# Halves of w1 by columns, and the second search's keys between row splits, in a routed expert kernel

## The chip, the cores and the metric

The kernel runs on one core of a Trainium2 chip. The core has five engines with a queue each: TensorE (PE, with its weight loads shown apart as PEld), VectorE (DVE), ScalarE (ACT), GpSimd (POOL) and SyncE (SP), and 16 DMA engines that they share. Each engine works through its own queue in the order in which the program was written, and waits at an instruction until what it needs is there. The metric is the time of one execution in device microseconds.

## The reference

The program computes an attention with a window of 32 and 32 global positions per head, and sends each of its 4608 rows of 512 numbers to one of eight experts. Each expert takes 576 rows: the highest gate values choose first, and who finds an expert full goes on.

```python
logits = x @ w_gate
order = np.argsort(-logits.flatten())
for idx in order:
    tok, e = (int(idx) // E, int(idx) % E)
    if assigned[tok] >= 0 or counts[e] >= cap:
        continue
    assigned[tok] = e
    counts[e] += 1
for e in range(E):
    mask = assigned == e
    h = np.maximum(x[mask] @ w1[e], 0.0)
    out[mask] = h @ w2[e]
```

w1 is 512 x 1024 and w2 1024 x 512 for each expert.

## The kernel before

**Stages.** Attention and the gate logits take the first 212 us and leave x in device memory (`xd`). Then the routing finds, one expert at a time, which expert fills first and which rows it gets. `search_alone` does this for the first expert with nothing beside it. `search` does it for each later one, in pieces that are laid between the matmuls of the expert that runs at that time. Before a search, `key` and `own` work out from the logits `L` what it compares: ten VectorE instructions that write r_m, r_v, r_f, r_v, r_u, r_mv, r_hi, r_G (these are `key`) and r_mo, r_oh (`own`). `key` is a generator that yields between five groups of them; `setup` runs `key` and then `own`. A search then does eight rounds: matmuls `R<-r_oh,r_G` on TensorE, r_ce on VectorE, matmuls with `big`, a scan r_pm, and the next r_G. At its end `widx` holds the row numbers for gathering this expert's weights, and a little later `idx` (made from the matmul `R<-c,r_w`) those of its token rows.

**An expert.** `ffn` computes with matmuls of float32r, each product as three: high x high, high x low and low x high parts. w1 is gathered into two tiles `w1r`, w2 into two tiles `w2r`, and the 576 token rows into five tiles `xg` (128, 128, 128, 128 and 32 rows), all by indirect DMAs that POOL issues (L895). A split takes a 128 x 512 piece: ACT copies it to the high part (w1h, w2h; L911) and VectorE subtracts to get the low part (w1l, w2l). w1 has eight pieces: j runs over 4 row blocks x 2 column halves, an even j being the first column half. `trans_x` transposes one row tile on TensorE, ACT makes xh from it (L936) and VectorE xl. For w1, eight column blocks f of 128 each, in two halves of rows, take 12 matmuls into an `H` tile (three buffers), from which ACT makes hh and VectorE hl. For f below 4 only the first column half of w1 is used. Then come the matmuls into `Y`, from which ACT makes y, and POOL scatters y to the output.

**What sets the order.** Within an expert, a table of due pieces (`at`, `step`, `force`) with an estimated clock of the program places splits, transpositions, gathers and the parts of the next search between the matmuls, when the program is built. The times it uses are constants in the code; `V.busy` and `V.now` are its estimates of where VectorE and TensorE stand. The pieces for even j carry the tag "a" and may come once the running expert is past its f = 4 (`half`), those for odd j the tag "b" and may come once it is done with w1. A piece of w1 is due when the gather it is read from is thought to have landed.

**Around the change.** w1 is stored so that each gather brings two of the four row blocks with all 1024 columns: pieces j = 0..3 read the first gather, j = 4..7 the second. For the first expert the order is written out at the end of `experts`: both w1 gathers as soon as `widx` is there, the row gathers after `idx`, both w2 gathers; on TensorE `HEAT` = 14 matmuls of `ident` with itself (`keep_warm`), then the five transpositions with three more such matmuls between them; on VectorE first the whole `setup` for the second search, then four w1l, then the xl. The odd pieces of w1 and all of w2 are left to the table.

Of the kernel before, what the change touches and what calls it, by code (L numbers as in the profile page):

```python
# [8 lines left out]
F32 = mybir.dt.float32  # L9
# [12 lines left out]
E = 8  # L22
FF = 1024
# [851 lines left out]
def experts(ctx, tc, A, xd, ident, rt, out):  # L875
    nc = tc.nc
    wp = ctx.enter_context(tc.tile_pool(name="wp", bufs=1))
    st = ctx.enter_context(tc.tile_pool(name="st", bufs=2))
    ps = ctx.enter_context(tc.tile_pool(name="fps", bufs=1, space=PSUM))
    w1h = [wp.tile([128, FF], F32R, name=f"w1h{c}") for c in range(4)]  # L880
    w1l = [wp.tile([128, FF], F32R, name=f"w1l{c}") for c in range(4)]
# [12 lines left out]
    def gather(dst, src, off, idx):  # L894
        nc.gpsimd.indirect_dma_start(out=dst, out_offset=None, in_=src, element_offset=off,  # L895
                                     in_offset=bass.IndirectOffsetOnAxis(ap=idx, axis=0))

    def load_w1(ph):
        raws = []
        for k in range(2):  # L900
            raw = st.tile([128, 2, FF], F32, name="w1r", bufs=2)
            gather(raw.rearrange("p a b -> p (a b)"), A["w1"], k * E * 128 * 2 * FF, rt.widx[ph][:, :1])
            raws.append(raw)
        return raws

    def load_w2(ph):
        for k in range(2):
            gather(w2r[k].rearrange("p a b -> p (a b)"), A["w2"], k * E * 128 * 4 * DM, rt.widx[ph][:, :1])

    def split(hi, lo, raw, eng):  # L910
        nc.scalar.activation(hi, raw, AF.Copy)  # L911
        eng.tensor_tensor(lo, raw, hi, op=ALU.subtract)

    def split_w1(raws, j, eng):
        q = slice(512 * (j % 2), 512 * (j % 2) + 512)
        split(w1h[j // 2][:, q], w1l[j // 2][:, q], raws[j // 4][:, (j // 2) % 2, q], eng)

    def split_w2(j, eng):
        split(w2h[j], w2l[j], w2r[j // 4][:, j % 4], eng)
# [1 line left out]
    def load_x(ph):  # L921
        xg = []
        for t in range(5):
            n = sizes[t]
            g = st.tile([128, DM], F32, name="xg", bufs=5)
            gather(g[:n], xd, 0, rt.idx[ph][:n, t:t + 1])
            xg.append(g)
        return xg

    def trans_x(xg, t):  # L930
        n = sizes[t]
        p = ps.tile([128, 4, 128], F32, name="H", bufs=3)
        for d in range(4):
            nc.tensor.transpose(p[:, d, :n], xg[t][:n, 128 * d:128 * d + 128], ident[:n, :n])  # L934
        q = slice(128 * t, 128 * t + n)
        nc.scalar.activation(xh[:, :, q], p[:, :, :n], AF.Copy)  # L936
        V.tensor_tensor(xl[:, :, q], p[:, :, :n], xh[:, :, q], op=ALU.subtract)
# [9 lines left out]
    fill, todo, raw1 = [], [], {}  # L947
    done, cur, mid, wrote = [False], [0], [-1], [0.0]

    def pool_op(ns, nbytes=0):  # L950
        pool[0] = max(pool[0], V.now) + ns
        if nbytes:
            dma[0] = max(dma[0], pool[0] + 1800) + nbytes / 360.0
            return dma[0] + 300
        return pool[0]

    def calm():
        return V.busy < V.now + AHEAD
# [13 lines left out]
    def at(tag, t, f, cond=None):  # L972
        todo.append((tag, t, cond, f))
# [27 lines left out]
    def low1(p, j):  # L1001
        split_w1(raw1[p], j, V)
# [2 lines left out]
        split_w2(j, V)  # L1005

    def get_w1(p, half):
        raw1[p] = load_w1(p)
        r = [pool_op(1040, 1 << 20) for _ in range(2)]
        for i in range(4):  # L1010
            at(f"a{p}", r[i // 2], lambda j=2 * i: low1(p, j), lambda: (half or mid[0] == p - 1) and calm())
        for i in range(4):
            at(f"b{p}", r[i // 2], lambda j=2 * i + 1: low1(p, j), lambda: mid[0] == p - 1 and calm())

    def get_x(p):
        xg = load_x(p)
# [22 lines left out]
    def ffn(ph):  # L1039
# [4 lines left out]
        if nxt < E:  # L1044
            at(f"g{nxt}", t0, lambda: get_w1(nxt, half), lambda: nxt in rt.widx and not pending(f"b{ph}"))
            at(f"h{nxt}", t0, lambda: get_x(nxt), lambda: nxt in rt.idx and (mid[0] == ph or V.now > t0 + TX))
            at(f"v{nxt}", t0, lambda: get_w2(nxt), lambda: mid[0] == ph and nxt in rt.widx and
               (not pending(f"h{nxt}") or V.now > t0 + TW))
# [54 lines left out]
    raws = None  # L1103
# [4 lines left out]
    def keep_warm(n):  # L1108
        for _ in range(n):
            nc.tensor.matmul(heat[:, :128], ident, ident, start=True, stop=True)  # L1110

    for _ in rt.phase(0):
        if raws is None and 0 in rt.widx:
            raws = load_w1(0)
    xg = load_x(0)
    load_w2(0)
    keep_warm(HEAT)
    raw1[0] = raws
    for _ in rt.setup(slice(0, 34)):
        pass  # L1120
    for j in range(4):
        split_w1(raws, 2 * j, nc.vector)
    for t in range(5):
        trans_x(xg, t)
        if t < 4:
            keep_warm(3)
    V.now = V.busy
    for j in range(4):
        at("b0", 0, lambda j=j: low1(0, 2 * j + 1), calm)
# [7 lines left out]
def _blocks(a, x, g):  # L1137
    pad = np.zeros_like(np.take(x, range(32), axis=a))
    bl = [pad] + np.split(x, NW, axis=a) + [pad]
    out = []  # L1140
    for i, b in enumerate(bl):
        out.append(b)
        if i % 2 == 0 and i < NW + 1:
            out.append(g)
    return np.concatenate(out, axis=a)


def _layout(q_l, k_l, v_l, q_g, k_g, v_g, moe_w_gate, moe_w1, moe_w2):
    f = np.float32
    qT = np.concatenate([q_l, q_g], axis=2).transpose(0, 1, 3, 2)  # L1150
    kT = _blocks(3, k_l.transpose(0, 1, 3, 2), k_g.transpose(0, 1, 3, 2))
    qk = np.concatenate([qT, kT], axis=3).reshape(B, NP, 2 * D, QW + KW)
    vs = _blocks(2, v_l, v_g)
    st = [32 * ((3 * j + 1) // 2) for j in range(NW)]
    vs = np.concatenate([vs, np.ones_like(vs[..., :1])], axis=3)
    vw = np.stack([vs[:, :, t:t + 128] for t in st[::2]], axis=3)
    vw = vw.reshape(B, NP, 2, 128, NW // 2, D + 1).transpose(0, 1, 3, 2, 4, 5).reshape(B, NP, 128, NW * (D + 1))
    w1 = moe_w1.reshape(E, 2, 2, 128, FF).transpose(1, 0, 3, 2, 4).reshape(2 * E * 128, 2 * FF)
    w2 = moe_w2.reshape(E, 2, 4, 128, DM).transpose(1, 0, 3, 2, 4).reshape(2 * E * 128, 4 * DM)
    wg = np.zeros((128, 4, 32), f)  # L1160
    wg[:, :, :E] = moe_w_gate.reshape(4, 128, E).transpose(1, 0, 2)[:, :, ::-1]
    mask = np.full((128, NB, 128), 0.0, f)
    i = np.arange(32)
    for j in range(NW):
        for w, bk in enumerate([j - 1, j, None, j + 1] if j % 2 else [j - 1, None, j, j + 1]):
            if bk is not None:
                t = 32 * bk + i
                ok = (np.abs(t[None] - 32 * j - i[:, None]) <= 32) & (t >= 0) & (t < SL)
                h = 32 * (j % 4)
                mask[h:h + 32, j // 4, 32 * w:32 * w + 32] = np.where(ok, 0.0, -3.0e37)  # L1170
    p = np.arange(128)
    cf = np.zeros((128, CF), f)
    cf[:, 0:8] = 1 + np.arange(8)
    cf[:, 13] = p + 1024
    ids = np.zeros((128, 34), int)
    for J in range(32):
        ids[:, J] = (J // 4) * S + SG + 128 * (J % 4) + p
    for J in (32, 33):
        ids[:, J] = (4 * (J - 32) + p // 32) * S + p % 32
    cf[:, 20:88] = np.stack([ids // 64, ids % 64], -1).reshape(128, 68)  # L1180
    cf[:, 88:216] = np.arange(128)[None]
    cf[:, 216:344] = -(p[:, None] >= p[None]).astype(f)
    cf[:, 344:472] = 1
    cf[:, 472:480] = (p[:, None] % 8 == np.arange(8)[None])
    cf[:, 480:512] = (p[:, None] % 32 == np.arange(32)[None])
    h = p % 16
    cf[:, 512:640] = (h[:, None] < 9) & (h[:, None] % 2 == np.arange(128)[None] // 64)
    cf[:, 640:645] = (h[:, None] // 2 == np.arange(5)[None]) * np.where(p % 32 < 16, 64, 1)[:, None]
    k = np.arange(16)
    for it in range(NIT):  # L1190
        cf[:, CTAB + 16 * it:CTAB + 16 * it + 16] = k * 16.0 ** (3 - it)
    cf[:, CFIN:CFIN + 128] = (256 + 16 * k[:, None] + 1 + np.arange(E)[None]).reshape(1, 128)
    cf[:, CMISC:CMISC + 32] = CU * (p[:, None] % 32 == np.arange(32)[None])
    a = dict(qk=qk, vw=vw, w1=w1, w2=w2, wg=wg.reshape(128, 128), mask=mask.reshape(128, 512),
             ident=np.eye(128, dtype=f), cf=cf)
    return {n: np.ascontiguousarray(x) for n, x in a.items()}
# [15 lines left out]
```

## Time and profile before

| what | value |
|---|---|
| median of 3 runs | 719.35 us (718.57 to 726.27) |
| profiled execution | 716.33 us |
| its span | 714.6 us, 23883 instructions |
| TensorE busy | 658.5 us, 92% |
| VectorE busy | 477.3 us, 67% |
| ScalarE busy | 320.8 us, 45% |
| GpSimd busy | 221.7 us, 31% |
| first expert matmul | 251.72 us |

The span is cut below by stretches of time. A group's busy time can hold overlaps, since a matmul's weight load and the end of the one before it run beside it; the start times of neighbouring rows tell the pace. A row of a timeline has the start in us, the length in us, the engine, the line, the instruction with output and inputs, how many were merged into it, and in brackets the idle time of the engine before it with what ended it. The name after an arrow in the brackets is the last releaser that the profile saw.

### The profile page before, as it was taken

The page shows a single profiled execution, that of the slowest core. Times are in us where ns is not written, and L with a number is a line of the kernel's source. Part 1 is how long each engine was busy: PE and PEld are TensorE (multiplying, and loading weights), DVE is VectorE, ACT ScalarE, POOL GpSimd, SP SyncE. Part 2 cuts the span into 40 slices and gives each one's busy share as a digit, 9 for nine tenths or more (in the row PEclk, how much of TensorE's full clock was granted, in tenths as well). Part 3 has the DMA queues.
Part 4 walks back from the last instruction along what each step waited for, and adds up shares of the span by engine and source line. Part 5 has one row for each costly group of instructions (what it writes and reads, how often), then busy time and mean ns, then how long its engine had stood idle before and what let it go on. Part 6 is the DMA issues. An engine that isn't in the chain of part 4 may idle for free.

```text
span 714.6 us, 23883 instructions
## 1 busy us (share of the span) xinstructions
PE 658.5 (92%) x9972; PEld 538.9 (75%) x9972; DVE 477.3 (67%) x1766; ACT 320.8 (45%) x870; POOL 221.7 (31%) x248
## 2 busy tenths in 40 slices
PE   7888898898993699999999999999999999999997
PEld 5666676676772598779789779878978877988985
DVE  3779777687777878767767777767776774640510
ACT  5867867776840243343244234234333342641421
POOL 3665546554510500430240241142043035312002
PEclk9999999999995599999999999999999999999999
DMA  8788878887310620730540351261063065331001
GB/s 281 244 270 274 273 247 258 282 268 246 134 68 2 216 84 1 266 96 2 209 139 17 144 177 42 86 213 66 2 241 121 2 250 177 116 118 49 16 16 48
DMA packets 39580, 102.86 MB, mean 144 GB/s; under 512 B 4912, under 2 KB 14384, under 8 KB 35376
## 3 DMA queue, kind: packets, MB, share of 16 engines
q1 hardware_dynamic: 29232, 49.95, 21.6%
q0 software_dynamic: 10240, 51.39, 20.4%
q8 instruction: 78, 1.28, 0.7%
q14 instruction: 30, 0.25, 0.1%
HBM read 83.49 MB, written 17.83 MB: 142 GB/s over the span
## 4 chain that ended last, share of the span: by engine, by line
PE 45%; DVE 4%; issue 3%; DMA 3%; POOL 1%; ACT 1%; POOLq 0%; DVEq 0%; ACTq 0%
PE Y L1090 19%; PE H L1062 19%; PE R L617 3%; PE H L934 2%; DVE w2l L546 2%; PE Y L1080 2%; DMA xg<-xd,idx 2%; DMA out_dram<-y,idx 1%; DVE r_G L546 1%; ACT w2h L911 1%; POOL xg L895 1%; DVE r_pm L546 0%; PE Y L1096 0%; DVE hl L546 0%; POOL w1r L895 0%
## 5 line engine op out<-in xcount | busy, mean ns | idle before, releaser
L1062 PE MATMUL H<-xh,w1h 128*128 128x272 f32 x512 | 151.3, 296 | 1.8 <-DVE hl L546 1.4
L1062 PE MATMUL H<-xh,w1l 128*128 128x272 f32 x512 | 150.1, 293 | 0.0
L1062 PE MATMUL H<-xl,w1h 128*128 128x272 f32 x512 | 149.9, 293 | 0.0
L1064 ACT ACTIVATE hh<-H 128x272 fp32r<-128x272 f32 x128 | 50.9, 398 | 130.1 <-PE H L1062 125.7
L1090 PE MATMUL Y<-w2h,hh 128*128 128x512 f32 x256 | 103.9, 406 | 0.0
L1090 PE MATMUL Y<-w2l,hh 128*128 128x512 f32 x256 | 102.7, 401 | 0.0
L1090 PE MATMUL Y<-w2h,hl 128*128 128x512 f32 x256 | 102.4, 400 | 0.0
L1062 PEld LDWEIGHTS H<-xh,w1h 128*128 128x128 f32 x512 | 96.5, 188 | 5.2 <-DVE hl L546 2.2
L1062 PEld LDWEIGHTS H<-xl,w1h 128*128 128x128 f32 x512 | 96.4, 188 | 0.6
L1062 PEld LDWEIGHTS H<-xh,w1l 128*128 128x128 f32 x512 | 96.4, 188 | 0.3
L941 POOL DMA_INDIRECT out_dram<-y,idx x40 | 40.2, 1006 | 137.4 <-ACT y L1032 79.3
L173 ACT ACTIVATE p<-p,nm 128x128 f32<-128x128 f32 x256 | 78.1, 397 | 10.4 <-DVE nm L168 10.4
L168 DVE CUSTOM_DVE_ANT_0 p<-S,mask 128x128 f32<-128x128 f32 x256 | 56.8, 286 | 28.0 <-PE S L83 25.9
L546 DVE SCALAR_TENSOR_TENSOR hl<-H,hh 128x272 fp32r<-128x272 f32 x128 | 54.4, 433 | 23.6 <-ACT h L1066 12.7
L546 DVE TENSOR_TENSOR w2l<-w2r,w2h 128x512 fp32r<-128x512 f32 x64 | 43.1, 686 | 37.4 <-ACT w2h L911 37.0
L895 POOL DMA_INDIRECT w1r<-in_w_dram,widx x16 | 15.7, 981 | 165.9 <-DVE r_a L546 124.3
L83 PE MATMUL S<-qk 64*32 64x128 f32 (+2 forms) x2240 | 53.9, 293 | 12.6 <-issue 6.1
L1032 ACT ACTIVATE y<-Y 128x512 f32<-128x512 f32 (+1 forms) x40 | 23.2, 594 | 92.1 <-PE Y L1090 65.9
L119 POOL COPY vw<-vw 64x1040 f32<-64x1040 f32 x32 | 33.6, 1049 | 88.3 <-DMA vw<-in_vw_dram 61.4
L1090 PEld LDWEIGHTS Y<-w2h,hh 128*128 128x128 f32 x256 | 48.2, 188 | 15.7 <-issue 5.9
L911 ACT ACTIVATE w1h<-w1r 128x512 fp32r<-128x512 f32 x64 | 36.4, 622 | 47.4 <-DVE r_ohg L546 27.5
L1090 PEld LDWEIGHTS Y<-w2h,hl 128*128 128x128 f32 x256 | 48.2, 188 | 10.1 <-issue 0.2
(176 smaller groups left out, 1215.7 us busy)
## 6 DMA issues: line engine op xcount, KB each, us to landing
vw<-in_vw_dram SPq DMA_DIRECT2D x64, 260.0 KB, 3.8
qk<-in_qk_dram SPq DMA_DIRECT2D x64, 216.0 KB, 3.5
qk<-in_qk_dram SPq DMA_DIRECT2D x32, 272.0 KB, 4.1
xd<-xs SPq DMA_DIRECT2D x28, 256.0 KB, 3.5
xd<-xs SPq DMA_DIRECT2D x1, 1024.0 KB
xg<-xd,idx POOLq DMA_INDIRECT x40, 3.6
out_dram<-y,idx POOLq DMA_INDIRECT x40, 2.7
cf<-in_cf_dram SPq DMA_DIRECT2D x1, 512.0 KB
```

The costliest lines, as they stand in the source:

```text
L83: s.last = op(o, w, x, **kw)
L119: nc.gpsimd.tensor_copy(od[0:64], ev[64:128])
L168: nc.vector.tensor_tensor_reduce(s.p[:, c, :], s.st[:, c, :], mask[:, c, :], -SCALE, BIG, ALU.add, ALU.min, s.nm[:, c:c + 1])
L173: nc.scalar.activation(s.p[:, c, :], s.p[:, c, :], AF.Exp, bias=s.nm[:, c:c + 1], scale=-1.0)
L546: return op(*args, **kw)
L895: nc.gpsimd.indirect_dma_start(out=dst, out_offset=None, in_=src, element_offset=off, in_offset=bass.IndirectOffsetOnAxis(ap=idx, axis=0))
L911: nc.scalar.activation(hi, raw, AF.Copy)
L941: nc.gpsimd.indirect_dma_start(out=out, out_offset=bass.IndirectOffsetOnAxis(ap=rt.idx[ph][:n, t:t + 1], axis=0), in_=y[:n], in_offset=None)
L1032: nc.scalar.activation(y[:n], p[:n], AF.Copy)
L1062: nc.tensor.matmul(p, w[d][:, fs], x[:, d, q], start=(d + k == 0), stop=(d + k == 5))
L1064: nc.scalar.activation(hh[:, f, q], p, AF.Relu)
L1090: nc.tensor.matmul(p, h[:, f, q], w[f], start=(f + k == 0), stop=(f + k == 9))
```

## The change

w1 is laid out in device memory so that the first gather brings the first 512 columns of all four row blocks, and the second the other 512. The even pieces j then read the first gather and the odd pieces the second, for every expert. For the first expert only the first gather is issued when `widx` is there; the second follows the five row gathers in POOL's queue, ahead of w2's. The second search's `setup` is no longer run ahead of the w1l subtractions: its first four steps go behind the first four row tiles, one each, and the rest behind the fifth. In the table the "a" pieces are due with the first gather and the "b" pieces with the second.

```diff
-    def load_w1(ph):
-        raws = []
-        for k in range(2):
-            raw = st.tile([128, 2, FF], F32, name="w1r", bufs=2)
-            gather(raw.rearrange("p a b -> p (a b)"), A["w1"], k * E * 128 * 2 * FF, rt.widx[ph][:, :1])
-            raws.append(raw)
-        return raws
+    def load_w1(ph, k):
+
+        raw = st.tile([128, 4, FF // 2], F32, name="w1r", bufs=2)
+        gather(raw.rearrange("p a b -> p (a b)"), A["w1"], k * E * 128 * 2 * FF, rt.widx[ph][:, :1])
+        return raw
...
-        split(w1h[j // 2][:, q], w1l[j // 2][:, q], raws[j // 4][:, (j // 2) % 2, q], eng)
+        split(w1h[j // 2][:, q], w1l[j // 2][:, q], raws[j % 2][:, j // 2], eng)
...
-        raw1[p] = load_w1(p)
+        raw1[p] = [load_w1(p, k) for k in range(2)]
         r = [pool_op(1040, 1 << 20) for _ in range(2)]
         for i in range(4):
-            at(f"a{p}", r[i // 2], lambda j=2 * i: low1(p, j), lambda: (half or mid[0] == p - 1) and calm())
+            at(f"a{p}", r[0], lambda j=2 * i: low1(p, j), lambda: (half or mid[0] == p - 1) and calm())
         for i in range(4):
-            at(f"b{p}", r[i // 2], lambda j=2 * i + 1: low1(p, j), lambda: mid[0] == p - 1 and calm())
+            at(f"b{p}", r[1], lambda j=2 * i + 1: low1(p, j), lambda: mid[0] == p - 1 and calm())
...
-            raws = load_w1(0)
+            raws = [load_w1(0, 0)]
     xg = load_x(0)
+    raws.append(load_w1(0, 1))
     load_w2(0)
     keep_warm(HEAT)
     raw1[0] = raws
-    for _ in rt.setup(slice(0, 34)):
-        pass
     for j in range(4):
         split_w1(raws, 2 * j, nc.vector)
+    setup = rt.setup(slice(0, 34))
     for t in range(5):
         trans_x(xg, t)
         if t < 4:
             keep_warm(3)
+            next(setup, None)
+    for _ in setup:
+        pass
     V.now = V.busy
```

Three places show what this does to the queues. The first is VectorE ahead of the first expert: r_G, r_mo and r_oh end the second search's keys, w1l are the low parts of w1's first column half, xl those of the row tiles. Before:

```order
L546 TENSOR_TENSOR r_G<-r_hi,cf 128x544
L546 SCALAR_TENSOR_TENSOR r_mo<-r_asgv,r_mv 128x34
L546 TENSOR_TENSOR r_oh<-r_v,r_mo 128x272
L912 TENSOR_TENSOR w1l_5374<-w1r,w1h_5370 128x512
L912 TENSOR_TENSOR w1l_5375<-w1r,w1h_5371 128x512
L912 TENSOR_TENSOR w1l_5376<-w1r,w1h_5372 128x512
L912 TENSOR_TENSOR w1l_5377<-w1r,w1h_5373 128x512
L546 TENSOR_TENSOR xl<-H,xh 128x4x128 x4
L546 TENSOR_TENSOR xl<-H,xh 128x4x32
```

The same place now, from behind the second row tile on:

```order
L546 TENSOR_TENSOR r_v<-L,r_m 128x272
L546 TENSOR_SCALAR r_f<-r_m 128x34
L546 TENSOR_TENSOR xl<-H,xh 128x4x128
L546 TENSOR_TENSOR r_v<-r_v,wtb 128x272
L546 TENSOR_TENSOR r_u<-r_f,r_m 128x34
L546 TENSOR_TENSOR xl<-H,xh 128x4x128
L546 TENSOR_REDUCE r_mv<-r_v 128x34
L546 TENSOR_SCALAR r_hi<-r_u 128x34
L546 TENSOR_TENSOR xl<-H,xh 128x4x32
L546 TENSOR_TENSOR r_G<-r_hi,cf 128x544
L546 SCALAR_TENSOR_TENSOR r_mo<-r_asgv,r_mv 128x34
L546 TENSOR_TENSOR r_oh<-r_v,r_mo 128x272
```

The keys moved from ahead of the w1l to between and behind the xl, and r_oh from ahead of everything to the end.

The second place is TensorE at the start of the first expert: the last transposition, the first expert matmuls (H), and the first matmul of the second search (R), which reads r_G and r_oh. Before:

```order
L1110 MATMUL Y<-ident 128x128 x3
L934 MATMUL H<-ident,xg 128x32 x4
L1062 MATMUL H<-xh,w1h_5370 128x272
L617 LDWEIGHTS r_G
L617 MATMUL R<-r_oh,r_G 32x16
```

Now:

```order
L932 MATMUL H<-ident,xg 128x32 x4
L1060 MATMUL H<-xh,w1h_5370 128x272
L1060 MATMUL H<-xl,w1h_5370 128x272
L1060 MATMUL H<-xh,w1l_5374 128x272
L1060 MATMUL H<-xh,w1h_5371 128x272
L617 LDWEIGHTS r_G
L617 MATMUL R<-r_oh,r_G 32x16
```

The search begins behind four expert matmuls instead of one.

The third place is ACT in the second expert's Y stage, where it makes the third expert's w1h between the evacuations y of the second. Before:

```order
L1032 ACTIVATE y<-Y 32x512
L911 ACTIVATE w1h_5370<-w1r 128x512
L911 ACTIVATE w1h_5371<-w1r 128x512
L911 ACTIVATE w1h_5372<-w1r 128x512
L911 ACTIVATE w1h_5373<-w1r 128x512
L1032 ACTIVATE y<-Y 128x512
```

Now:

```order
L1030 ACTIVATE y<-Y 32x512
L909 ACTIVATE w1h_5370<-w1r 128x512
L909 ACTIVATE w1h_5371<-w1r 128x512
L909 ACTIVATE w1h_5372<-w1r 128x512
L1030 ACTIVATE y<-Y 128x512
L909 ACTIVATE w1h_5373<-w1r 128x512
```

One split moved behind the next y; in the first expert's Y stage, where the fourth split stood behind that y, the third now does too. From the third expert on the later experts' Y stages repeat, in the main, the order that the expert before them had, and in the sixth expert's the row gathers of the seventh go ahead of its w2 gathers in POOL's queue.

More of the change, by code (lines that the diff above doesn't have):

```diff
@@ L1157, in _layout @@
     vw = vw.reshape(B, NP, 2, 128, NW // 2, D + 1).transpose(0, 1, 3, 2, 4, 5).reshape(B, NP, 128, NW * (D + 1))
-    w1 = moe_w1.reshape(E, 2, 2, 128, FF).transpose(1, 0, 3, 2, 4).reshape(2 * E * 128, 2 * FF)
+    w1 = moe_w1.reshape(E, 4, 128, 2, FF // 2).transpose(3, 0, 2, 1, 4).reshape(2 * E * 128, 2 * FF)
     w2 = moe_w2.reshape(E, 2, 4, 128, DM).transpose(1, 0, 3, 2, 4).reshape(2 * E * 128, 4 * DM)
```

## The prediction

> **What bounds the kernel now.** I read the page's busy shares first, then the table of busy time by stretch, then TensorE's waits, and last the timeline around the start of the first expert. The stretch rows give the span's start and end, its length, then busy us (and instructions) of PE, PEld, DVE, ACT and POOL, the granted clock, the DMA share and GB/s.
> ```profile
> 240.87:251.72 10.85, 10.85 (x73) 10.69 (x72) 8.20 (x20) 4.07 (x8) 5.81 (x7) 0.73 0.80 270
> 251.72:714.60 462.88, 452.85 (x3814) 377.99 (x3812) 290.82 (x772) 167.51 (x400) 105.08 (x103) 1.00 0.29 103
> ```
> ```profile
> PE H L934 <- DMA xg<-xd,idx: 1.5, 2, 1.1
> PE H L1062 <- DVE hl L546: 1.4, 5, 0.5
> PE R L617 <- DVE r_G L546: 1.1, 3, 0.4
> ```
> From 251.72 us, where the first expert's matmuls begin, TensorE is busy 452.85 of 462.88 us at full clock: 97.8%. Its waits that the profile names there (us in total, times, longest) come to 4.0 us. So behind 251.72 no edit that leaves the matmuls alone can win over 10 us, and by the named waits not over 4.0. An added wait in TensorE's queue, on the other hand, goes straight to the end. The question is what happens at 240.87 to 254, which the change rewrites.
> ```profile
> 240.87 6.13 PE L1110 MATMUL Y<-ident 128*128 128x128 f32 x28
> 246.84 0.60 PE L934 MATMUL H<-ident,xg 128*128 128x128 f32 x4
> 251.36 0.43 PE L934 MATMUL H<-ident,xg 32*128 32x32 f32 x4
> 251.72 0.39 PE L1062 MATMUL H<-xh,w1h 128*128 128x272 f32 x1
> 252.04 0.28 PE L617 MATMUL R<-r_oh,r_G 128*32 128x16 f16 x17
> 252.26 0.40 PE L1062 MATMUL H<-xl,w1h 128*128 128x272 f32 x1
> 252.74 0.29 PE L1062 MATMUL H<-xl,w1h 128*128 128x272 f32 x1
> ```
> TensorE (start, length, instruction) runs the 14 warming matmuls (28 records) without a break from 240.87 to the first row transposition at 246.84, and no idle time stands in any of these rows: nothing that arrives earlier can start the transpositions earlier, because the warming matmuls stand ahead of them in the queue and are not changed. The first part of the second search (R) runs at 252.04 behind one expert matmul.
>
> **The gathers.** The landing rows give minimum, median and maximum from issue, first for w1's two gathers of the first expert, then for the row gathers up to 262 us.
> ```profile
> 234.20 1.17 POOL L895 DMA_INDIRECT w1r<-in_w_dram,widx  x1 [0.78 <-POOL widx L766]
> 235.68 0.95 POOL L895 DMA_INDIRECT w1r<-in_w_dram,widx  x1 [0.31 <-issue]
> 246.30 0.96 POOL L895 DMA_INDIRECT w2r<-in_w_dram,widx  x1 [0.30 <-issue]
> DMA to landing us min/median/max: 5.8/7.0/8.2
> DMA to landing us min/median/max: 3.0/3.7/4.7
> ```
> ```profile
> 240.25 1.15 ACT L911 ACTIVATE w1h<-w1r 128x512 fp32r<-128x512 f32 x2 [27.51 <-DVE r_ohg L546]
> 243.89 1.15 ACT L911 ACTIVATE w1h<-w1r 128x512 fp32r<-128x512 f32 x2 [2.49 <-DMA w1r<-in_w_dram,widx]
> 252.00 1.14 ACT L911 ACTIVATE w1h<-w1r 128x512 fp32r<-128x512 f32 x2
> 253.95 0.40 ACT L1064 ACTIVATE hh<-H 128x272 fp32r<-128x272 f32 x1 [0.80 <-PE H L1062]
> ```
> Each gather still moves 128 rows of 2048 numbers, so bytes and rows per gather are the same: cost 0. The first lands at 240.2, when ACT starts on it, and the second at 243.9. Now all four first-half splits hang on the first, so ACT does them from 240.25 to about 242.6 instead of finishing at 245.04. The row gathers pass the second one in POOL's queue and no longer queue behind its bytes. They need not be sooner: TensorE is in the warming matmuls until 246.84. Gain 0. The second w1 gather takes the place where w2's first stood, 246.30; with the 5.8 us of an undisturbed landing it is there at 252.1, where ACT started on that half at 252.00 anyway; with the 8.2 us of a queued one, 254.5. Behind it on ACT stands the first hh, at 253.95 before, and TensorE has three H buffers, 24 matmuls of lead after the first group, so 254.5 is still covered; cost 0, price if it landed after about 257 one us for each us. w2 comes one gather later, with eight f steps of cover: 0.
>
> **The moved keys.** VectorE before, start, length, instruction:
> ```profile
> 241.38 0.42 DVE L546 TENSOR_REDUCE r_m<-L 128x34 f32<-128x272 f32 x1
> 243.21 0.72 DVE L546 TENSOR_TENSOR r_G<-r_hi,cf 128x544 f16<-128x544 int32 x1
> 244.07 0.44 DVE L546 TENSOR_TENSOR r_oh<-r_v,r_mo 128x272 f16<-128x272 bf16 x1
> 244.54 2.50 DVE L912 TENSOR_TENSOR w1l<-w1r,w1h 128x512 fp32r<-128x512 f32 x4
> 248.16 0.69 DVE L546 TENSOR_TENSOR xl<-H,xh 128x512 fp32r<-128x512 f32 x1 [1.12 <-ACT xh L936]
> 249.21 0.69 DVE L546 TENSOR_TENSOR xl<-H,xh 128x512 fp32r<-128x512 f32 x1 [0.36 <-ACT xh L936]
> 251.43 1.00 DVE L546 TENSOR_TENSOR xl<-H,xh 128x512 fp32r<-128x512 f32 x2 [0.41 <-ACT xh L936]
> ```
> The ten key instructions, r_m to r_oh, ran from 241.38 to 244.51, while VectorE had nothing else: seven of them take 243.21 - 241.38 = 1.83 us, the last three (r_G, r_mo, r_oh) 244.51 - 243.21 = 1.30. That cover is given up. The four w1l subtractions now come first (241.45 to about 244.0) and VectorE then stands idle until the first xl at 248.16, where TensorE's pace puts it as before. From there its queue holds xl, key, xl, key and so on. Without any idle time: three xl of 2.50/4 = 0.62, the last two 1.00, the seven keys 1.83, together 4.70, hence 252.87; then the last three, 1.30: r_oh is ready at 254.17. That is the lower bound. If no key fitted into the idle 0.36 to 0.41 us between the xl, all ten would stand behind 252.43, the end of the last xl: 255.56. I take 254.17, since each piece of key (1.83/4 = 0.46) is about as long as the gap it goes into, with little left over. The expert's first matmuls need only the first three row tiles, done at about 251.0: no delay there.
>
> In TensorE's queue the search's first part now stands behind four expert matmuls and waits for r_G and r_oh. What follows it waits too, as this place in the second expert shows:
> ```profile
> 315.39 0.79 DVE L546 SCALAR_TENSOR_TENSOR r_G<-r_hi,r_pm,cf 128x544 f16<-128x544 int32 x1
> 316.23 0.28 PE L617 MATMUL R<-r_oh,r_G 128*32 128x16 f16 x17 [0.44 <-DVE r_G L546]
> 316.44 0.39 PE L1062 MATMUL H<-xh,w1l 128*128 128x272 f32 x1
> ```
> r_G ends at 316.18, R starts 0.05 later, the next expert matmul 0.21 after that; none went ahead. Here then R starts at 254.22 and the fifth expert matmul at 254.43. Before, the fifth was the row at 252.74. Added: 1.7 us, with 1.7 + 1.4 = 3.1 as the other end; a gain at this place is excluded, since r_oh cannot be earlier than its queue.
>
> **Later experts.** The first gather alone now serves all four "a" splits. At the end of the first expert:
> ```profile
> 297.01 0.60 ACT L1032 ACTIVATE y<-Y 128x512 f32<-128x512 f32 x1 [0.48 <-PE Y L1090]
> 298.16 0.69 DVE L546 TENSOR_TENSOR w1l<-w1r,w1h 128x512 fp32r<-128x512 f32 x1 [0.91 <-ACT w1h L911]
> 298.98 0.15 DVE L546 CAST idx<-R 128x5 int32<-128x5 f32 x1
> 300.68 2.29 POOL L895 DMA_INDIRECT xg<-xd,idx  x1 [0.30 <-issue]
> ```
> ```profile
> 297.05 0.18 PE L617 MATMUL R<-c,r_w 128*128 128x5 bf16 x1
> 302.69 0.66 PE L934 MATMUL H<-ident,xg 128*128 128x128 f32 x4
> 305.35 0.66 PE L934 MATMUL H<-ident,xg 128*128 128x128 f32 x4 [1.08 <-DMA xg<-xd,idx]
> ```
> The index matmul was done at 297.23, but idx was cast at 298.98, behind a w1l whose w1h stood on ACT behind a y that itself came from TensorE. So the row gathers were late and TensorE waited 1.08. Now two of the four splits stand behind that y (0.6 later on VectorE), while the transpositions stand four Y matmuls further on; 23 Y matmuls lay in 302.69 - 297.05 = 5.64 us, so 0.98. Net gain 0.98 - 0.6 = 0.4, bounds 0 and 1.08. In the second expert's end the y now goes ahead of the fourth split and the transpositions come 23 Y matmuls after the index matmul instead of 26: the pattern that waited 1.08 before. The 2.29 us gather was part of that wait and need not recur: bounds 0 and 1.1, taken 0.6. The pattern of the other wait on rows (0.4 of the 1.5) moves one expert on: 0. For the seventh expert the transpositions come 19 Y matmuls behind their index matmul instead of behind the last search: 19 x 0.245 = 4.7 us against a landing of 3.0 to 4.7 plus an issue: 0 to 0.8, taken 0.3.
>
> **Sum.** 1.7 - 0.4 + 0.6 + 0.3 = +2.2 us. The profiled execution took 716.33 us for a span of 714.6; the span becomes 716.8, the execution 718.5. The three runs shown have their median 3.0 above that execution, at 719.35, so the forecast on that scale is 721.6 us. A measurement here tells about 1%, 7 us, from no change: the forecast is no change, on the slow side.
>
> **Rivals.** (1) The chain at the start absorbs the delay: the keys fit wholly under the transpositions and the search's wait is under 0.5 us, while the first expert's row wait goes. Then 719.35 + 0.5 - 1.1 = 718.8. The idle 0.36 to 0.41 us on VectorE speak for it, r_G to r_oh behind the last xl (1.30) against. (2) Rows that land earlier start the first expert earlier, by up to the 3.65 us between the two w1 landings: 715.7 us. The unbroken 28 records to 246.84 speak against it; it needs the warming matmuls to have been waiting in disguise. (3) Slower: in the new wait TensorE's clock falls.
> ```profile
> 212.25:212.50 0.25, 0.25 (x3) 0.23 (x3) 0.00 (x0) 0.00 (x0) 0.00 (x0) 1.00 1.00 377
> 212.50:212.75 0.25, 0.01 (x1) 0.03 (x1) 0.00 (x0) 0.20 (x1) 0.00 (x0) 0.59 0.89 336
> ```
> The clock fell within the quarter us in which TensorE first went idle, so idle time of 2 us is enough to think of it. Coming back took from 240.87 to about 246.8 before, 6 us at half speed, that is 3 us lost: 721.6 + 3 = 724.6 us. It decides for slower by over 1% only if the fall comes twice or the wait is beyond 4 us. Against it: the 1.08 us wait at 305 left the clock at 1.00. The Trainium skill, "TensorE: Matmul & The Clock Gate", Part 1, says that the clock is halved after at least one idle window of about 3.4 us; by that rule a 2 us wait costs nothing more and the sum stays 721.6. The trace does not bear it out to the letter, as the fall at 212.5 came behind records that count TensorE as busy 0.25 of 0.25.
>
> **Chances.** Forecast 0.62 (its own range 719.5 to 723.5); rival 1 0.18; rival 2 0.05; rival 3 0.15, a third of it beyond 1%. The range from 717.5 to 725.0 leaves out rival 2 and the far part of rival 3, and takes in the bounds 3.1 and 0 of the two large terms. Faster by over 1% 0.02, within 1% 0.93, slower 0.05.
>
> **What would show it.** In the changed profile: warming matmuls still unbroken to the first transposition near 246.8; a wait of some 2 us of the first R on r_oh, near 252 to 254; r_oh ending near 254.2; ACT starting the second-half splits near 252; a wait on rows near the end of the second expert. I am wrong if that R does not wait, if the transpositions start before 246, or if the clock's row shows less than 1.0 after 247.

## The result, and the profile after

The changed kernel takes 726.49 us (median of 20 runs, 721.80 to 729.05) against 720.68 us (20 runs) for the kernel before, measured beside it: 1.0081 times the time, interval 1.0063 to 1.0099. The forecast was 721.6 over 719.35, a ratio of 1.0031, with an upper end of 725.0. So it is slower by 0.8%, on the side forecast, but by 5.8 us where 2.2 were worked out, and 1.5 us above the range. Most of that 1.5 is the base: the three runs shown had their median at 719.35, the twenty beside the changed kernel at 720.68, so that as a ratio the upper end (725.0 over 719.35, 1.0079) lies just under what was measured. The 5.8 against 2.2 does not depend on this.

The profiled execution of the changed kernel took 728.11 us for a span of 726.3. It is 1.6 us above its kernel's median, and the profiled one before (716.33) is 4.4 below the median of the twenty. The two profiles therefore lie 11.8 us apart where the medians lie 5.8 apart: they show where waits stand, and the sizes have to come from the experiments.

The busy times by stretch, cut again at the first warming matmul and at the first expert matmul (columns as before):

```profile
242.11:254.05 11.94, 10.89 (x74) 10.66 (x73) 5.77 (x13) 4.03 (x9) 7.01 (x8) 0.76 0.72 229
254.05:726.30 472.25, 455.06 (x3812) 378.84 (x3812) 292.62 (x779) 166.53 (x399) 104.79 (x103) 1.00 0.29 102
```

The warming started 1.24 us later than in the profile before, with nothing changed ahead of it: that is a difference of executions. The stretch from there to the first expert matmul is 1.09 longer (11.94 against 10.85). Everything behind it is 9.37 longer (472.25 against 462.88), and TensorE is busy 2.2 of these more: the rest, 7.2, is waiting. TensorE's waits from 254 us on (total us, times, longest) name it:

```profile
PE H L932 <- DMA xg<-xd,idx: 3.7, 4, 1.2
PE R L617 <- DVE r_oh L546: 2.0, 1, 2.0
PE R L617 <- DVE r_G L546: 1.5, 5, 0.4
PE R L617 <- DVE r_ce L546: 1.5, 1, 1.5
PE H L1060 <- DVE xl L546: 1.0, 1, 1.0
PE R L617 <- DVE r_ohl L546: 0.9, 1, 0.9
PE H L1060 <- DVE hl L546: 0.7, 3, 0.3
PE R L617 <- DVE r_cs L546: 0.6, 1, 0.6
```

Before there were three such lines with 4.0 us; here the eight come to 11.9 (with the 1.0 for xl, which lies just ahead of 254.05). One of them was forecast at its place and about its size, the wait for r_oh. The 1.5 for r_ce, at 552.87 in the fifth period, does not come back in every profile with these queues (see what is open). The start on TensorE, and then on VectorE:

```profile
242.11 6.10 PE L1108 MATMUL Y<-ident 128*128 128x128 f32 x28
248.05 0.60 PE L932 MATMUL H<-ident,xg 128*128 128x128 f32 x4
...
254.05 0.39 PE L1060 MATMUL H<-xh,w1h 128*128 128x272 f32 x1 [1.05 <-DVE xl L546]
...
256.80 0.27 PE L617 MATMUL R<-r_oh,r_G 128*32 128x16 f16 x17 [1.99 <-DVE r_oh L546]
...
257.01 0.39 PE L1060 MATMUL H<-xl,w1h 128*128 128x272 f32 x1
```

```profile
242.95 2.50 DVE L910 TENSOR_TENSOR w1l<-w1r,w1h 128x512 fp32r<-128x512 f32 x4 [0.27 <-issue]
249.37 0.69 DVE L546 TENSOR_TENSOR xl<-H,xh 128x512 fp32r<-128x512 f32 x1 [3.92 <-issue]
...
251.81 0.69 DVE L546 TENSOR_TENSOR xl<-H,xh 128x512 fp32r<-128x512 f32 x1 [1.41 <-ACT xh L934]
...
255.45 0.71 DVE L546 TENSOR_TENSOR r_G<-r_hi,cf 128x544 f16<-128x544 int32 x1
...
256.30 0.44 DVE L546 TENSOR_TENSOR r_oh<-r_v,r_mo 128x272 f16<-128x272 bf16 x1
```

The warming matmuls are unbroken again, and the first transposition comes 5.94 us behind their start (5.97 before). VectorE is idle for 3.92 us ahead of the first xl, where the keys used to be, and r_oh comes last. R stands ready at 254.8 and starts at 256.80, and the next expert matmul only behind it. That is the forecast's wait. The late second xl (1.41 idle) is not part of the forecast, and it pushes r_oh back too; more on it below. What followed the wait shows in the granted clock, in two stretches that end and begin where it changed:

```profile
254.66:258.08 3.42, 1.43 (x28) 1.35 (x27) 3.35 (x12) 0.30 (x1) 0.00 (x0) 1.00 0.90 376
258.08:261.49 3.41, 3.41 (x18) 3.29 (x17) 2.64 (x5) 0.97 (x3) 0.00 (x0) 0.50 0.00 0
```

TensorE was busy 1.43 of 3.42 us, and ran the next 3.41 at half clock. Expert matmuls follow each other every 0.225 us there instead of every 0.125, so these 3.41 us do the work of 1.9 and lose 1.5.

### The profile page after: what moved, and what is told of

The parts are those of the page before. It is cut to its first block, busy times and chain, and to the rows that moved or that the text cites. A ratio compares the mean times of both kernels' runs of the same rounds, so it can differ in the third digit from the quotient of the medians.

```text
span 726.3 us, 23885 instructions
## 1 busy us (share of the span) xinstructions
PE 661.1 (91%) x9972; PEld 539.9 (74%) x9972; DVE 477.3 (66%) x1766; ACT 319.8 (44%) x870; POOL 221.6 (31%) x248
## 5 line engine op out<-in xcount | busy, mean ns | idle before, releaser
L895 POOL DMA_INDIRECT xg<-xd,idx x40 | 43.0, 1075 | 54.6 <-DVE idx L546 40.1
```

## The experiments

Kernels that stand in one group were measured on the same chip together with the kernel before, whose median is given; the groups differ in that median by up to 4.5 us, so only ratios are compared across them. "Period" is the time from the first H matmul of one expert's w1 to that of the next, read from TensorE's timeline.

### First group (before: 716.97 us): the parts alone

start_only: the changed kernel, with the planner's clock set back, so that every queue behind the start stands as before. With it R stands behind one expert matmul again, as before, and not behind four.

```diff
         pass
     V.now = V.busy
+    rt.when = 0.0
```

> The changed kernel with the second search's first part put back behind one expert matmul in the program's table, so that all later queues stand as in the kernel before; the moved keys, the column halves and the order of the first gathers stay. Theory 1 (the loss is made at the start: TensorE waits for xl and then for r_oh, and its clock falls in that wait): slower than before by 3 to 5.5 us, the first search matmul waits about 2 us for r_oh, the way from the first warming matmul to the second expert's first matmul is 75 to 78 us against 72.1 before. Theory 2 (the loss is made by the shifted table in later experts): within 1.5 us of before, and that way 72 to 74 us.

Measured: 719.75 us, 1.0032 (1.0000 to 1.0065), that is 2.3 us by the ratio, between what the two theories said; the way to the second expert's first matmul is 74.15 us. R waits much as in the changed kernel (its row in TensorE's timeline), and the clock falls behind it (two stretches of busy time):

```profile
253.95 0.27 PE L617 MATMUL R<-r_oh,r_G 128*32 128x16 f16 x17 [1.90 <-DVE r_oh L546]
```

```profile
252.00:255.41 3.41, 1.51 (x29) 1.52 (x29) 3.30 (x12) 1.20 (x3) 0.00 (x0) 1.00 0.92 346
255.41:258.83 3.42, 3.42 (x18) 3.30 (x17) 2.02 (x4) 0.40 (x1) 0.00 (x0) 0.50 0.83 333
```

table_only: the kernel before, its start untouched, with the planner's clock moved to where the changed kernel has it. All queues behind the start stand as in the changed kernel, except for the gathers' halves.

```diff
         if t < 4:
             keep_warm(3)
     V.now = V.busy
+    rt.when = V.ready()
```

> The kernel before, with the second search's first part put behind four expert matmuls in the table, as the changed kernel has it; keys, halves and gathers are as before. All later queues stand as in the changed kernel. Theory 1: within 1.5 us of before, no wait of the first search matmul. Theory 2: slower than before by 3 to 6 us; the waits of the row transpositions for their rows in the second, third, sixth and seventh expert come to 3 to 5 us, as in the changed kernel's profile, against 1.5 before.

Measured: 719.65 us, 1.0028 (0.9993 to 1.0063), 2.0 us, which by itself is not clear of noise. No wait at the start; behind it waits for r_ohl in two experts (1.12 and 0.86 us) and for rows at the end of the first, the second and the sixth (0.98, 1.01 and 0.50).

keys_first (all keys ahead of the w1l as before) and keys_mid (all between the w1l and the first row tile): halves of w1 and the late second gather stay, the table is as before.

```diff
     for j in range(4):
         split_w1(raws, 2 * j, nc.vector)
-    setup = rt.setup(slice(0, 34))
+    for _ in rt.setup(slice(0, 34)):
+        pass
     for t in range(5):
         trans_x(xg, t)
         if t < 4:
             keep_warm(3)
-            next(setup, None)
-    for _ in setup:
-        pass
```

That is keys_mid; in keys_first the two new lines stand ahead of the w1l loop.

> The changed kernel with the second search's keys ahead of the first w1l again, as before; column halves and the second half's gather behind the row gathers stay. Queues stand as in the kernel before but for three gathers. Theory 1 and theory 2 both: within 1.5 us of before. A rival (theory 3: the later gather of w1's second half and the rows themselves are what is late, seen in xh of the second row tile 1.4 us behind its transposition): slower than before by 2 to 4 us, with that gap and the wait for xl still there.

> The changed kernel with all of the second search's keys between the four w1l and the first xl, where VectorE stood idle for 3.9 us; the table is that of the kernel before. Theory 1: the keys, 3.1 us, fit in the idle time, no wait for r_oh: equal to before within 1.5 us. Theory 2: the same. Theory 3: slower by 2 to 4 us, since the rows are still late. TensorE's warming matmuls still end about 6 us after they begin, so no gain.

Measured: 717.06 us, 1.0005 (0.9972 to 1.0037), and 716.84 us, 1.0001 (0.9975 to 1.0028). Reading w1 by halves and fetching the second half behind the rows neither gains nor costs more than these intervals leave room for, about 0.4%, and the keys may stand on either side of the w1l. The loss lies in the two other parts.

### Second group (before: 716.39 us): filling the wait, shifting further

after_warm: the changed kernel with eight warming matmuls ahead of the R that waits (rt.warm is run by the search just ahead of its first matmul).

```diff
+        s.warm = []
...
+            if s.warm:
+                s.warm.pop()()
...
+    rt.warm.append(lambda: keep_warm(8))
```

> The changed kernel with eight of the warming matmuls put between the fourth expert matmul and the first search matmul that waits, so that TensorE is not idle while it waits for r_oh. The eight take about 2 us, as long as the wait, and nothing else moves. If the fall of TensorE's clock to half after that wait (3.4 us at half speed in both profiles that had the wait) is part of the loss: the clock stays at 1.00 behind 248 us, and the time is 1 to 2 us less than the changed kernel's ratio to before, about +0.5% instead of +0.8%. If the fall costs nothing or comes from something else: the clock still falls, or the ratio stays at +0.8%.

Measured: 720.70 us, 1.0033 (1.0003 to 1.0062). The sixteen records fill the gap, and R waits no more:

```profile
254.84 1.95 PE L1111 MATMUL Y<-ident 128*128 128x128 f32 x16
256.72 0.28 PE L618 MATMUL R<-r_oh,r_G 128*32 128x16 f16 x17
```

The clock stayed at 1.00. The changed kernel itself, run once beside it (after_again), took 718.93 us, 1.0035 times that group's before: so no gain is shown.

> The changed kernel unchanged, for a second profile. What belongs to the program returns: the wait of the first search matmul of 1.9 to 2.0 us for r_oh, the fall of the clock behind it, waits of about 1 us for rows in the second and third expert. What was chance in the first profile does not: the second row tile's xh 1.85 us late and the 1.05 us wait for xl.

Its profile has the wait for r_oh (1.53 us, less than the 1.9 to 2.0 expected) with no fall of the clock behind it, and no late second row tile. The row waits at the end of the first and second expert are 0.93 and 0.96 us.

table_more: as table_only, with 0.8 us more.

```diff
+    rt.when = V.ready() + 800
```

> The kernel before, with the second search's start in the table moved by 0.8 us more than in the changed kernel; start and gathers as before. It asks whether it is this shift or any shift that costs. If any shift of the search against the expert costs (it comes later, and its rows with it): slower than before by 2 us or more. If it is a matter of how the pieces happen to fall: anything from 1 us faster to 3 us slower, with other waits than in the changed kernel, and E1 to E6 stretches that differ by up to 2.5 us each from before, of both signs.

Measured: 717.39 us, 0.9977 (0.9948 to 1.0006). A later clock in the planner is not dear in itself.

keys_mid_heat10: keys_mid with four warming matmuls fewer, to use the rows that land earlier.

```diff
-HEAT = 14
+HEAT = 10
```

> Keys between the w1l and the xl, and 10 warming matmuls instead of 14, which takes 4 x 0.43 = 1.7 us at half clock out of TensorE's queue. If the warming matmuls are what sets the start: the first expert matmul comes 1 to 1.7 us earlier after the first warming matmul (10.6 us in the run with 14), and the time falls by 1 to 1.7 us below before. If rows or keys set it: no gain. If the clock then rises later: a loss of up to 2 us.

Measured: 718.36 us, 1.0004 (0.9967 to 1.0042). The first expert matmul came 9.55 us behind the start of the warming instead of 10.57 in keys_mid, but then a search matmul waited 1.51 us for r_ce, and the first period was 62.68 instead of 61.54: what was gained ahead of it was lost in it.

### Third group (before: 720.84 us): the sizes once more

mid_table and mid_more are keys_mid with table_only's and table_more's line; start_warm is start_only with after_warm's eight matmuls, which here stand behind the first expert matmul, where start_only has R, and not behind the fourth; after_third is the changed kernel.

> The changed kernel with the second search's keys all ahead of the row tiles (between the low parts of w1 and the first row tile) and with the changed kernel's table behind it, so that the wait of the first search matmul at the start is gone and only the later queues differ from before. Theory (the shifted table costs by itself, by the wait of the R matmul on r_ohl in the first expert and row waits in the second and the last but one): ratio 1.002 to 1.004, that is +1.5 to +3 us, and a wait of about 1 us on r_ohl between 290 and 300 us. Rival (the 1.0028 of the kernel with the table alone was noise and the later queues cost nothing): 1.000, at most 1.001.

Measured: 725.82 us, 1.0069 (1.0043 to 1.0096): the shifted table alone costs, and more than expected. The wait for r_ohl was not in the first expert, as expected, but in the second (0.84 us).

> The same kernel, but the table is shifted 0.8 us further. Theory (it is not the shift but where the fourth r_ohl falls behind a low part of w1 that costs): the wait on r_ohl is under 0.5 us and the ratio 0.996 to 1.000, below the kernel with the smaller shift by 0.2% to 0.6%. Rival (any later search start costs): 1.002 to 1.005, not below the kernel with the smaller shift.

Measured: 721.08 us, 1.0008 (0.9975 to 1.0040). The wait for r_ohl is 0.36 us, and the further shift is below the smaller one by 0.6%, which is what the theory said; its reason, r_ohl, turns out to be the smaller part of it (below).

> The changed start with the later queues of before, and eight warming matmuls between the fourth expert matmul and the first search matmul, which waits. Theory (half of the start's cost is the clock, which falls to half speed behind the wait for 3.4 us, that is 1.7 us lost, in most executions): no wait over 0.5 us at that R, no granted clock under 1.00 behind 247 us, ratio 1.001 to 1.002 against 1.0032 without the warming matmuls. Rival (the cost is the wait alone): the warming matmuls only fill it, ratio 1.003 as without them.

Measured: 724.92 us, 1.0062 (1.0030 to 1.0093), well above both theories. The clock stayed at 1.00, and R still waited 0.57 us for r_oh. The profile has other waits, for r_ce (1.47 and 0.81), r_ohl (0.87) and xl (1.05), that start_only's does not have. So what the clock alone is worth in the median stays open.

> The changed kernel once more, nothing altered, beside the three others. Theory (start and table both cost, the start partly by the clock): ratio 1.006 to 1.010; in the profile a wait of 1.5 to 2.0 us of the first search matmul on r_oh, followed by a granted clock of 0.5 for about 3.4 us in some executions and not in others. Rival (the first measurement of it was high by chance): 1.003 or less.

Measured: 727.63 us, 1.0104 (1.0058 to 1.0149), with a wait of 1.99 us for r_oh and 3.4 us at half clock behind it.

All four profiles of this group, like the first one of the changed kernel, show the second row tile late on ACT: in mid_more the high parts (xh) of the first two row tiles and the expert's first matmul were

```profile
249.00 0.60 ACT L934 ACTIVATE xh<-H 128x512 fp32r<-128x512 f32 x1 [4.05 <-issue]
251.78 0.60 ACT L934 ACTIVATE xh<-H 128x512 fp32r<-128x512 f32 x1 [2.19 <-PE H L932]
...
255.33 0.39 PE L1060 MATMUL H<-xh,w1h 128*128 128x272 f32 x1 [1.74 <-DVE xl L546]
```

though TensorE's second transposition had begun at 249.42 and lasted 0.60. Whether this belongs to the change was one of the two questions for the last group.

### Fourth group (before: 716.91 us): repeats

before_again is the kernel before, keys_mid_2, start_only_2 and table_only_2 are the kernels of those names.

> The kernel before, unaltered. If the late second row tile on ACT belongs to the session and not to the change, it shows here as well whenever it shows in the others of this call: first expert matmul 11.8 us behind the first warming matmul instead of 10.85, with a wait of 1.0 to 1.7 us for xl. If it comes with the second gather of w1 behind the rows, it is absent here and 10.6 to 10.9 stand. Ratio 1.000 in either case.

> Halves of w1 and the late second gather kept, keys all ahead of the row tiles, table as before. Theory (these parts cost nothing in any session): ratio 0.998 to 1.002. Rival (they bring the late second row tile in some sessions): 1.002 to 1.004 in a session in which that wait shows, and the wait for xl ahead of the first expert matmul in its profile, not in that of the kernel before.

> The changed start with the later queues of before. Theory (wait of the first search matmul for r_oh, 1.5 to 2 us, and behind it the clock in some executions): 1.002 to 1.004 in a session without the late second row tile, 1.004 to 1.007 in one with it. Rival (the first 1.0032 was chance): 1.000 to 1.001.

> The kernel before with the shifted table alone. Theory (the shifted table costs by itself through r_ohl and the row waits): 1.002 to 1.005. Rival (1.0028 was chance, and the 1.0069 of the kernel with the halves and the shifted table came from the session): 1.000 to 1.001.

Measured: 0.9999 (0.9966 to 1.0032), 1.0004 (0.9974 to 1.0035), 1.0045 (1.0011 to 1.0078) and 1.0069 (1.0037 to 1.0100). Start and table each cost, in a second measurement too, now clear of noise. Together, 1.0032 to 1.0045 and 1.0028 to 1.0069, they are as large as the loss of the changed kernel, 1.0081 and 1.0104. None of the four profiles has the late row tile, so this group does not say whether the kernel before would have it: open. In before_again the first expert matmul came 9.71 us behind the first warming matmul, not the 10.6 to 10.9 expected, because its clock rose after 3.4 us of warming instead of 5.8.

start_only_2 had the same wait as start_only, 1.90 us, and no fall of the clock. Again the two stretches, on the clock's own grid of 3.41 us (here placed by the moment at which it rose during the warming):

```profile
247.63:251.04 3.41, 1.86 (x31) 1.86 (x32) 3.26 (x10) 1.15 (x2) 0.00 (x0) 1.00 0.94 360
251.04:254.45 3.41, 3.41 (x45) 3.24 (x44) 2.20 (x5) 1.40 (x4) 0.00 (x0) 1.00 0.56 231
```

Its first period is 63.24 us against 64.61 in start_only: 1.37 us for the clock, near the 1.5 worked out above, and 1.90 over the 61.34 of before_again for the wait.

## Why the prediction fell short

**What was right.** The warming matmuls hide any earlier rows: unbroken, and in the changed kernel's profile the same distance to the first transposition. The gathers cost nothing (keys_first and keys_mid 1.0005, 1.0001 and 1.0004). The first search matmul waits for r_oh at the forecast place, 1.5 to 2.0 us in five profiles against a term of 1.7. Only after_again (1.53) has it under the forecast's own conditions: the two waits of 1.99 go with the late second row tile, and the two of 1.90 are start_only's, with one expert matmul ahead of R instead of four. The moment of r_oh was a matter of the clock: in start_only it rose earlier in the warming than in the profile before, so that the first expert matmul came 9.54 us behind the start of the warming instead of 10.85 and r_oh ended 11.78 behind it instead of the 13.30 forecast; both moved together, and the time from one to the other hardly did (2.24 against 2.45).

**What went to a rival.** The clock fell behind that wait in three of the five profiles, as the third rival had it, which held 0.15. It cost 1.4 to 1.5 us rather than 3. Taken with the wait, the start costs 1.0032 and 1.0045: 2.3 and 3.2 us where the sum had 1.7. The rule of the Trainium skill, "TensorE: Matmul & The Clock Gate", Part 1, that one idle window of about 3.4 us halves the clock, was read as if a wait under 3.4 us were safe. Here half clock followed a window that was busy 42 to 44%, and not one busy 54 to 55%.

**The step that failed** is "Later experts", -0.4 + 0.6 + 0.3 = +0.5 us. The shifted table alone measured 1.0028, 1.0069 and (on the changed gathers) 1.0069, that is 2 to 5 us, though the first of these is not clear of noise. The periods of table_only_2 against before_again, without any difference at the start, give +3.4 us over the seven:

| period | 1 | 2 | 3 | 4 | 5 | 6 | 7 |
|---|---|---|---|---|---|---|---|
| before_again | 61.34 | 59.25 | 58.75 | 58.02 | 58.78 | 59.27 | 52.38 |
| table_only_2 | 61.02 | 60.44 | 59.27 | 58.76 | 57.96 | 62.09 | 51.67 |
| after | 65.59 | 60.17 | 59.25 | 58.76 | 59.66 | 62.15 | 52.00 |
| mid_more | 59.29 | 60.33 | 60.49 | 59.26 | 58.75 | 59.21 | 52.31 |

The largest term by far is the seventh expert's, in period 6: 2.8 us where 0.3 was taken (0.7 of it comes back in period 7). In table_only period 6 was 60.73, 1.5 us longer. In the kernel before, the index matmul of that expert, its idx and its row gathers stood ten us ahead of the transposition. First the kernel before, then the changed one:

```profile
588.14 0.18 PE L617 MATMUL R<-c,r_w 128*128 128x5 bf16 x1
588.89 1.17 POOL L895 DMA_INDIRECT xg<-xd,idx  x1 [1.90 <-DVE idx L546]
599.20 0.60 PE L934 MATMUL H<-ident,xg 128*128 128x128 f32 x4
```

```profile
595.71 0.18 PE L617 MATMUL R<-c,r_w 128*128 128x5 bf16 x1
596.87 0.69 DVE L546 TENSOR_TENSOR w1l<-w1r,w1h 128x512 fp32r<-128x512 f32 x1 [1.44 <-ACT w1h L909]
597.48 0.16 DVE L546 CAST idx<-R 128x5 int32<-128x5 f32 x1
597.90 1.47 POOL L895 DMA_INDIRECT xg<-xd,idx  x1 [10.68 <-DVE idx L546]
599.57 0.18 PE L617 MATMUL R<-r_cs,cb 128*128 128x34 bf16 x1 [0.62 <-DVE r_cs L546]
601.69 0.66 PE L932 MATMUL H<-ident,xg 128*128 128x128 f32 x4 [0.42 <-DMA xg<-xd,idx]
607.82 0.63 PE L932 MATMUL H<-ident,xg 128*128 128x128 f32 x4 [1.22 <-DMA xg<-xd,idx]
```

The forecast counted 4.7 us of Y matmuls against the landing plus an issue, for the first row tile alone, and that tile's wait, 0.42, is near the 0.3 taken. What it left out came on top. It left out that the idx cast stands on VectorE behind a w1l, which waits for a w1h that ACT makes behind a y: 1.6 us from the end of the index matmul to the cast. It had used just this pattern for the first expert, a few lines earlier. And it left out the fourth row tile (1.22) and r_cs in the same VectorE queue (0.62). The three waits are 2.26 us. All seven profiles with these later queues have the wait for r_cs (0.62 or 0.63) and one of 0.40 to 0.53 for the first row tile, and five of them one of 1.1 to 1.3 for the fourth; none of the other profiles has one of 0.3 us or more at these places. No run put these gathers back alone, so their price is read from the traces and not tested by itself.

The first expert's row wait was to shrink by 0.4 and did not: 1.02 us, for in the changed order idx was cast at 306.74, again behind a w1l. The second expert's came at 1.07 (0.87 to 1.09 in the seven profiles), at the upper bound of 1.1 instead of the 0.6 taken; the row there is

```profile
372.48 0.66 PE L932 MATMUL H<-ident,xg 128*128 128x128 f32 x4 [1.07 <-DMA xg<-xd,idx]
```

And a wait that the forecast had not looked for stands in the first expert of the changed kernel (in the second one in mid_table and after_third). ACT, VectorE and TensorE:

```profile
300.20 1.15 ACT L909 ACTIVATE w1h<-w1r 128x512 fp32r<-128x512 f32 x2 [3.38 <-DMA w1r<-in_w_dram,widx]
300.86 0.69 DVE L546 TENSOR_TENSOR w1l<-w1r,w1h 128x512 fp32r<-128x512 f32 x1 [2.89 <-ACT w1h L909]
301.47 0.43 DVE L546 TENSOR_TENSOR r_ohl<-r_hb,tab 128x544 bf16<-128x544 bf16 x1
301.96 0.80 PE L617 MATMUL R<-r_ohl,rhs 128*32 128x64 bf16 x20 [0.92 <-DVE r_ohl L546]
```

One r_ohl stands behind a w1l, whose w1h waits for the first w1 gather. That gather came 7.0 us after its issue at 293.17 here. It varies from one execution to the next, 5.4 to 7.2 us at this place and the next expert's, and in the changed queues a wait of 0.8 to 1.1 us for r_ohl came with each landing of 6.9 or more (7.0 here, 7.2 in table_only and after_again, 6.9 in the second expert of mid_table and after_third); in table_only_2 it took 5.6 both times, there was no such wait, and that execution was still 0.5% above the median of before. The queues of before are not safe from it either: start_warm, which has them, waited 0.87 behind a landing of 6.5. So this is a part of the loss that comes and goes, and the rows of the second and the seventh expert are, but for the fourth row tile, the part that stays.

That it is these places and not the later clock as such is what mid_more and table_more speak for: 0.8 us more of shift, period 6 back at 59.21 and 58.67, and 1.0008 and 0.9977 where the smaller shift has 1.0069 and 1.0028. Their waits for r_ohl were 0.36 and 0.37 us, though the gather took 7.0, and neither has the seventh expert's three waits. They are no clean test, since with the further shift every period changes: period 1 is about 2 us shorter than before, periods 2 to 4 are 1.1 to 1.9 longer.

**What is open.** Why that gather's landing varies. Why the second row tile was late in five profiles, four of them of one group: it is 1.1 of the 9.4 + 1.1 us that the profile of the changed kernel lost behind the start of its warming. The 1.51 us wait for r_ce in that profile is of the same kind, TensorE's results taken up late by both other engines at once. These are TensorE's, VectorE's and ACT's rows there:

```profile
548.39 0.28 PE L617 MATMUL R<-r_oh,r_G 128*32 128x16 f16 x17
549.40 0.60 PE L932 MATMUL H<-ident,xg 128*128 128x128 f32 x4
552.39 0.42 DVE L546 TENSOR_TENSOR r_ce<-R,dk 128x256 f16<-128x256 f32 x1 [2.50 <-PE H L932]
552.48 1.09 ACT L934 ACTIVATE xh<-H 128x512 fp32r<-128x512 f32 x2 [3.62 <-PE H L932]
```

after_third and mid_table wait at the same instruction (1.47 and 1.44); after_again, after_warm and both runs of table_only, with the same queues, do not, so the order alone does not make it. The two groups in which these late starts appear are those in which the kernel before itself has a median of 720.7 and 720.8 us; in the other three it is 716.4 to 717.0. That speaks for the session more than for the change, but the profile of the kernel before, whose three first times are among the twenty of 720.7, shows neither. And it is open how much the warming matmuls are worth: after_warm and start_warm held the clock, but their ratios (1.0033 beside 1.0035, and 1.0062) show no gain.

## What to carry to other kernels

When work moves in a queue, follow the engine that makes the moved transfer's address as closely as the transfer: a cast of two tenths of a microsecond, behind a split that hung on another engine, held the row gathers back by 1.6 us here. A wait added in front of a saturated TensorE is paid in full (1.90 us of wait made the first period 1.90 longer in start_only_2), and may be paid again in clock (1.4 to 1.5 us). Filling the wait kept the clock up here, but no gain in time was shown. A planner's order should be tried at a few neighbouring starts before a change that shifts it is judged, since 0.8 us of shift moved this kernel by half a per cent.

## What the runs showed of the hardware

In all eighteen traces every stretch between two changes of the granted clock lasts a multiple of 3.41 us: the clock changes on a grid. A wait of 1.90 to 1.99 us that fell into one cell of it (TensorE busy 1.42 to 1.51 us of 3.41) was followed by 3.41 us at half clock, in start_only, after and after_third. The same wait of 1.90 us across two cells (start_only_2, busy 1.86 of 3.41 in the one that holds most of it), and 1.53 us in after_again (1.88), were not. This gives no sharp threshold: in the attention stage cells busy 1.71 us (mid_more, from 69.34 us) and 1.85 us (after_third, from 178.05) were followed by half clock, and cells busy 1.52 us (after_third, from 113.20) and 1.64 us (keys_mid_2, from 116.19) were not.

At half clock expert matmuls followed each other every 0.225 us instead of every 0.125, less than twice. And in the warming stretch the rise came 3.1 us behind its start in start_only, 5.7 in after and 5.8 in before: the start of the expert's matmuls moves with it by over a microsecond from one execution to the next (9.54 us behind the first warming matmul in start_only, 10.85 in before). The change itself moved it far less: 9.71 us in before_again and 9.76 in after_again, where the rise came after 3.4 and 3.5.
